# Interleaving the first two feed-forward blocks of a linear-attention and FFN kernel while its weights are converted

## The chip, the cores and the metric

One core of one Trainium2 chip. The metric is the time of one execution on the device in microseconds (us), as the median of several runs. Some executions of a kernel can be slower, at a lower clock. Each experiment ran on one chip with runs of the kernel before; not all used the same chip. The *granted clock* is the share of TensorE's full clock that the profile shows as granted to it. A ratio is the mean time of one kernel's fast runs over that of the other's of the same rounds, so it is not quite the ratio of the medians quoted beside it; the interval is 95%.

## The reference

```python
# attention: batch 4, heads 8, seq 768, head_dim 48
f = 1.0 / (1.0 + np.exp(-f_logit))
for t in range(S):
    state = f[:, :, t, :, None] * state + np.einsum('bhd,bhe->bhde', k[:, :, t], v[:, :, t])
    y[:, :, t] = np.einsum('bhd,bhde->bhe', q[:, :, t], state)
# feed-forward: 3072 tokens, d_model 384, d_ff 1536
a = x @ w_a
b = x @ w_b
return (a * b @ w_out).astype(np.float32)      # x is y, heads side by side
```

The three weights arrive in double precision and are brought to single precision on the chip.

## The kernel before

The names that matter. A *block* is 384 tokens; there are eight. A *unit* is four heads of a block; units 0 and 1 make block 0, and so on up to unit 15. The weights come in 36 *pieces* of 128 x 384: twelve of w_b and twelve of w_a in turn, then twelve of w_out. A piece passes ScalarE and GpSimd, then four instructions on VectorE. An *input set* holds the input tiles of one unit. A feed-forward block has twelve *up steps* (b-half, a-half, product `ab` on VectorE), each of which needs one piece of w_b and one of w_a, and then three *down groups* of twelve matmuls, which need w_out. (Each matmul makes two records in a profile. In the kernel before, block 0 takes the 36 down matmuls as twelve groups of three instead.) In the code NFT is 12 and NTG is 3, so a block has 15 steps.

A unit passes through `front` (three parts, split by `yield`: ScalarE and GpSimd; long scans on VectorE; short scans and the products of q and k on VectorE), `scores` (48 small matmuls that need the scaled k, then a mask on VectorE), `turn`, `gains`, `within` and `across`. Instructions stand on each engine in program order, so the text below is the schedule. From unit 2 on a `slot` spreads these parts between the up steps and down groups:

```python
def slot(u):
    nxt = front(u + 1) if u + 1 < NU else iter(())
    if u > NQ:                   # NQ = 2
        within(u - 1)
    if u < NU:
        scores(u)
    yield
    next(nxt, None)              # front of u + 1, first part
    yield
    if u < NU:
        turn(u)
    yield
    next(nxt, None)              # second part
    yield
    ...                          # across(u - 1), gains(u)
    yield
    next(nxt, None)              # last part: k of u + 1
    yield
```

The start and the main loop, cut:

```python
for names in ("f", "kqv"):
    for u in range(NQ):
        for n, eng, x in (("f", nc.vector, 30.0), ("k", nc.gpsimd, 0.0), ("q", nc.vector, 0.0)):
            if n in names:
                eng.memset(sets[u][n], x)
        load_unit(u, names)
for ps in (ps_x, ps_y):
    nc.vector.memset(ps, 0.0)
...                              # units 0 and 1, pieces 1 and 2, front of unit 2
convert(4)
queue = []
for s in slots:
    for d in (0, 1, 2.2, 3.4, 4.6, 5.8)[1 if s == NQ else 0:]:
        queue.append(((s - NQ) * (NFT + NTG) / 2 - 6 + d, s))      # one slot in 7.5 steps
queue.sort(reverse=True)
for blk in range(NBLK):
    for i in range(10**6):
        step = blk * (NFT + NTG) + (min(i, NFT) + max(i - NFT, 0) / 4 if blk == 0 else i)
        while queue and queue[-1][0] <= step:
            next(slots[queue.pop()[1]], None)
        if i == 0:
            part = ffn(blk)      # one up step or down group at each next(part)
        if blk == 0:
            convert(min(2 * i + 4, 2 * NFT) if i < NFT - 1 else NFT + i + 3)
        if next(part, "end") == "end":
            break
```

So block 0 alone runs during the conversion; its down groups follow the pieces of w_out one by one.

## Time and profile before

| | before |
|---|---|
| time, median of 4 runs | 706.44 us (706.01 to 706.95) |
| span of the profiled run, granted TensorE clock | 703.4 us, 0.968 |
| last piece of w_out converted | 159.5 us |
| TensorE gapless from | 163.06 us |

The page's slices, the busy time by stretch and the end of the first stage are shown in the prediction. The timeline of TensorE in the kernel before, scores alone (start, length, engine, line, operation, tiles, shapes, count; in brackets the idle time before it and what ended it):

```profile
42.85 1.66 PE L277 MATMUL ps_x<-q_in,k_in 48*64 48x64 f32 x48 [8.48 <-DVE k_in L249]
60.14 0.88 PE L277 MATMUL ps_x<-q_in,k_in 48*64 48x64 f32 x48
108.04 1.56 PE L277 MATMUL ps_x<-q_in,k_in 48*64 48x64 f32 x48 [7.12 <-DVE k_in L249]
167.73 0.88 PE L277 MATMUL ps_x<-q_in,k_in 48*64 48x64 f32 x48
198.88 0.93 PE L277 MATMUL ps_x<-q_in,k_in 48*64 48x64 f32 x48
```

Units 2 and 4 find TensorE waiting; unit 3 and those from 5 on do not. Where it waited, the 48 matmuls take 1.6 us instead of 0.9: they run at half the clock (from 108.04 to 109.53 us the granted clock is 0.50).

### The profile page before, as it was taken

How to read it: one execution, taken by the hardware profiler on the slowest of the kernel's cores; microseconds unless marked ns; L12 is line 12 of the kernel's file. 1: busy time of each engine (PE TensorE's matmuls, PEld its weight loads, DVE VectorE, ACT ScalarE, POOL GpSimd, SP SyncE). 2: the span in 40 equal slices, each digit the busy share in tenths (PEclk: the TensorE clock that was granted, in tenths of full speed). 3: DMA queues.
4: the chain of work that ended last, by engine and by line, in shares of the span. 5: the costliest groups of instructions: out<-in, count | busy, mean ns of one | idle time of the engine just before them, and what ended most of it. 6: DMA issues, size and time to landing. Idle time of an engine off the chain costs nothing.

```text
span 703.4 us, 11473 instructions
## 1 busy us (share of the span) xinstructions
PE 640.7 (91%) x4770; PEld 389.9 (55%) x4770; DVE 278.9 (40%) x566; ACT 177.9 (25%) x343; POOL 76.2 (11%) x110
## 2 busy tenths in 40 slices
PE   1519868789999999999999999999999999999996
PEld 1415435346666666666666656566666665555553
DVE  8679999994343124231434024231514111001100
ACT  2543665652221022112121122112121021101100
POOL 6333443530000000000000000000000000000000
PEclk9858988999999999999999999999999999999999
DMA  9972365451030403040121203040000000000000
GB/s 205 234 202 69 112 171 143 131 132 55 10 77 18 101 1 86 1 107 12 32 55 48 71 1 86 0 107 12 18 2 29 23 1 18 20 33 0 1 12 26
DMA packets 34301, 43.30 MB, mean 62 GB/s; under 512 B 4032, under 2 KB 32704, under 8 KB 34240
## 3 DMA queue, kind: packets, MB, share of 16 engines
q1 hardware_dynamic: 24224, 29.60, 16.9%
q10 hardware_dynamic: 10016, 12.88, 6.2%
q8 instruction: 39, 0.64, 0.4%
q14 instruction: 22, 0.18, 0.1%
HBM read 33.03 MB, written 4.72 MB: 54 GB/s over the span
## 4 chain that ended last, share of the span: by engine, by line
PE 78%; DVE 13%; DMA 4%; ACT 2%; issue 1%; ACTq 1%; POOL 0%; SPq 0%; DVEq 0%; POOLq 0%
PE f L418 48%; PE f L438 24%; DVE r L193 3%; DVE h L189 2%; DVE r L192 2%; DVE f_in L237 1%; PE ps_y L356 1%; PE ps_y L376 1%; PE ps_x L277 1%; PE ps_x L304 1%; DMA raw<-in_moe_w_b_dram 1%; PE ps_x L323 1%; DVE w_b L195 1%; DVE inv L247 1%; DMA v_in<-in_v_dram 1%
## 5 line engine op out<-in xcount | busy, mean ns | idle before, releaser
L418 PE MATMUL f<-xT,w_b 128*128 128x384 f32 x576 | 209.7, 501 | 6.9 <-ACT b_sb L426 6.9
L418 PE MATMUL f<-xT,w_a 128*128 128x384 f32 x576 | 202.6, 488 | 0.0
L438 PE MATMUL f<-w_out,ab 128*128 128x384 f32 x576 | 192.1, 492 | 5.9 <-ACT b_sb L426 3.0
L428 DVE TENSOR_TENSOR ab<-f,b_sb 128x384 f32<-128x384 f32 x96 | 53.5, 557 | 308.8 <-PE f L418 307.6
L438 PEld LDWEIGHTS f<-w_out,ab 128*128 128x128 f32 x576 | 109.2, 191 | 83.7 <-DVE w_out L195 5.4
L418 PEld LDWEIGHTS f<-xT,w_a 128*128 128x128 f32 x576 | 110.5, 192 | 77.7 <-issue 2.4
L418 PEld LDWEIGHTS f<-xT,w_b 128*128 128x128 f32 x576 | 108.3, 194 | 78.7 <-ACT b_sb L426 9.8
L426 ACT COPY b_sb<-f 128x384 f32<-128x384 f32 x96 | 46.0, 479 | 243.3 <-PE f L418 236.3
L448 ACT COPY o_sb<-f 128x384 f32<-128x384 f32 x24 | 11.5, 479 | 175.3 <-PE f L438 173.9
L232 POOL TENSOR_SCALAR inv<-inv 128x768 f32<-128x768 f32 x16 | 15.0, 937 | 369.2 <-ACT inv L230 369.2
L277 PE MATMUL ps_x<-q_in,k_in 48*64 48x64 f32 x720 | 15.7, 239 | 30.0 <-DVE k_in L249 15.6
L183 POOL TENSOR_SCALAR h<-h 128x384 f32<-128x384 f32 x36 | 25.9, 720 | 66.5 <-ACT h L177 66.0
L277 PEld LDWEIGHTS ps_x<-q_in,k_in 48*64 48x64 f32 x720 | 13.9, 151 | 30.8 <-DVE k_in L249 15.9
L237 DVE TENSOR_TENSOR_SCAN f_in<-f,zero 128x384 f32<-128x384 f32 x32 | 29.9, 974 | 1.7 <-ACT inv L230 1.7
L339 DVE TENSOR_TENSOR st<-st,ps_x 128x96 f32<-128x96 f32 x80 | 20.3, 253 | 24.3 <-PE ps_x L323 21.8
L177 ACT ACTIVATE h<-raw 128x384 f32<-128x384 f32 x36 | 20.0, 557 | 38.5 <-DVE r L193 24.8
L387 ACT COPY y<-ps_y 64x384 f32<-64x384 f32 (+1 forms) x48 | 22.8, 475 | 18.5 <-PE ps_y L376 16.0
L184 POOL TENSOR_SCALAR h<-h 128x384 uint16<-128x384 uint16 x36 | 27.0, 751 | 3.0
L247 DVE TENSOR_TENSOR_SCAN inv<-inv,start,zero 128x128 f32<-128x128 f32 x64 | 26.9, 461 | 0.0
L193 DVE SCALAR_TENSOR_TENSOR r<-raw,r 128x384 f32<-128x384 uint32 x36 | 24.8, 690 | 1.2
L180 ACT ACTIVATE bit<-sign 128x384 uint16<-128x384 f32 x36 | 22.9, 636 | 1.3
L189 DVE SCALAR_TENSOR_TENSOR h<-h,bit 128x384 uint32<-128x384 uint32 x36 | 21.0, 584 | 1.3 <-POOL h L184 1.3
(60 smaller groups left out, 303.0 us busy)
## 6 DMA issues: line engine op xcount, KB each, us to landing
f_in<-in_f_logit_dram SPq DMA_DIRECT2D x32, 144.0 KB, 3.0
k_in<-in_k_dram SPq DMA_DIRECT2D x32, 144.0 KB, 3.5
q_in<-in_q_dram SPq DMA_DIRECT2D x32, 144.0 KB, 3.9
v_in<-in_v_dram SPq DMA_DIRECT2D x16, 288.0 KB, 4.3
raw<-in_moe_w_out_dram ACTq DMA_DIRECT2D x12, 384.0 KB, 3.1
out_dram<-o_sb SPq DMA_DIRECT2D x24, 192.0 KB, 1.9
raw<-in_moe_w_b_dram ACTq DMA_DIRECT2D x10, 384.0 KB, 3.5
raw<-in_moe_w_a_dram ACTq DMA_DIRECT2D x10, 384.0 KB, 3.3
```

What stands on the lines that cost most here:

```text
L180: nc.scalar.activation(bit.bitcast(U16).rearrange("p (n two) -> p n two", two=2)[:, :, 1], sign, AF.Relu, scale=-32768.0)
L183: nc.gpsimd.tensor_scalar(h, h, HI_MAX, HI_MIN, ALU.min, ALU.max)
L184: nc.gpsimd.tensor_scalar(upper, upper, 1.0, -float(HI_BIAS), ALU.mult, ALU.add)
L189: nc.vector.scalar_tensor_tensor(out=hu, in0=hu, scalar=3, in1=bit, op0=ALU.logical_shift_left, op1=ALU.bitwise_or)
L193: nc.vector.scalar_tensor_tensor(out=r, in0=lo, scalar=2.0**-52, in1=r, op0=ALU.mult, op1=ALU.mult)
L237: nc.vector.tensor_tensor_scan(x[:, c], f[:, c], none, math.exp(MIDDLE), ALU.mult, ALU.add)
L247: nc.vector.tensor_tensor_scan(inv[:, w], inv[:, w], none[:, 0:C], first, ALU.mult, ALU.add)
L277: nc.tensor.matmul(ps[h][SUB * p:SUB * p + SUB, o:o + SUB], lhsT=kf[r, tokens(n, c, p)], rhs=qf[r, tokens(n, c, p)], start=True, stop=True,)
L418: nc.tensor.matmul(ps[nm], lhsT=w[:, kt, ft * 128:ft * 128 + 128], rhs=x[:, kt], start=kt == 0, stop=kt == NKT - 1,)
L426: nc.scalar.copy(b_sb, ps["b"])
L428: nc.vector.tensor_tensor(ab[ft], ps["a"], b_sb, ALU.mult)
L438: nc.tensor.matmul(o[tg], lhsT=ab[ft][:, tg * 128:tg * 128 + 128], rhs=w_out[:, ft], start=ft == 0, stop=ft == NFT - 1,)
```

## The change

Its intent is to run up steps of blocks 0 and 1 in turn while pieces are converted, so that two converted columns of w_a and w_b serve two up steps instead of one and TensorE has work during the conversion of w_out. For it, units 2 and 3 (block 1) move ahead, units 4 to 6 get slots at steps 12, 18 and 24, three input sets take the place of four (with single buffers for `at`, `kT`, `y`, to make room for more `ab`), and the start gives VectorE's clearing to GpSimd and ScalarE. Cut to its core:

```diff
-    NSET = 4
+    NSET = 3
...
-        for ps in (ps_x, ps_y):
-            nc.vector.memset(ps, 0.0)
+        for n, x in (("f", 30.0), ("k", 0.0), ("q", 0.0)):
+            for u in range(NSET):
+                eng = nc.vector if n == "f" or n == "q" and u == 0 else nc.gpsimd
+                eng.memset(sets[u][n], x)
+        for ps in (ps_x, ps_y):
+            nc.scalar.copy(ps[:, :, 0:BLK], zero.unsqueeze(1).broadcast_to((128, 2, BLK)))
...
         across(1)
+        convert(4)
+        up(0, 0)
         next(fronts[2])
         next(fronts[2])
-        slots = {s: slot(s) for s in range(NQ, NU + 1)}
-        next(slots[NQ])
-        convert(4)
+        next(fronts[3])
+        next(fronts[3])
+        scores(2)
+        turn(2, True)
+        within(2)
+        next(fronts[3])
+        gains(2)
+        up(0, 1)
+        scores(3)
+        across(2)
+        turn(3, True)
+        convert(6)
+        up(0, 2)
+        within(3)
+        gains(3)
+        convert(8)
+        up(0, 3)
+        across(3)
+        convert(10)
+        up(0, 4)
+        rest = [(up, blk, i + 5 * (1 - blk)) for i in range(7) for blk in (1, 0)]
+        rest += [(up, 1, i) for i in range(7, NFT)]
+        rest += [(down, blk, tg) for blk in range(2) for tg in range(NTG)]
...                                  # then blocks 2 to 7, each ups then downs
+        first = {2 * NQ: 12, 2 * NQ + 1: 18}
+        queue = [(2 * NQ + 5, fronts[2 * NQ]), (2 * NQ + 6.5, fronts[2 * NQ]), (2 * NQ + 7.5, fronts[2 * NQ])]
         for s in slots:
-            for d in (0, 1, 2.2, 3.4, 4.6, 5.8)[1 if s == NQ else 0:]:
-                queue.append(((s - NQ) * (NFT + NTG) / 2 - 6 + d, s))
+            for d in (0, 1, 2.2, 3.4, 4.6, 5.8):
+                queue.append((first.get(s, (s - NQ) * (NFT + NTG) / 2 - 6) + d, slots[s]))
...
+        for step, (what, blk, i) in enumerate(rest, 5):
+            while queue and queue[-1][0] <= step:
+                next(queue.pop()[1], None)
+            convert(10 + (step - 4) * 3 // 2)
+            what(blk, i)
```

More of the change, by code (lines that the diff above doesn't have):

```diff
@@ L89, in by_quotients @@
     NBLK = B * NH
-    NSET = 4
+    NSET = 3
     fixedp = ctx.enter_context(tc.tile_pool(name="fixed", bufs=1))
+    sb1 = ctx.enter_context(tc.tile_pool(name="sb1", bufs=1))
     sb2 = ctx.enter_context(tc.tile_pool(name="sb2", bufs=2))
-    sb4 = ctx.enter_context(tc.tile_pool(name="sb4", bufs=4))
-    ab_pool = ctx.enter_context(tc.tile_pool(name="ab", bufs=NFT + 1))
+    sb3 = ctx.enter_context(tc.tile_pool(name="sb3", bufs=3))
+    ab_pool = ctx.enter_context(tc.tile_pool(name="ab", bufs=2 * NFT + 1))
     raw_pool = ctx.enter_context(tc.tile_pool(name="raw", bufs=5))
@@ L114, in by_quotients @@
     less = fixed([128, 1], "less")
-    signs = [
-        (fixed([128, PIECE], f"sign{i}"), fixedp.tile([128, PIECE], U32, tag=f"bit{i}", name=f"bit{i}"))
-        for i in range(3)
-    ]
+    sign = fixed([128, PIECE], "sign")
+    bits = [fixedp.tile([128, PIECE], U32, tag=f"bit{i}", name=f"bit{i}") for i in range(3)]
     tails = fixed([128, NU], "tails")
@@ L171, in from_double @@
         lo, hi = words[:, :, 0], words[:, :, 1]
-        i = nth[0] % len(signs)
+        bit = bits[nth[0] % len(bits)]
         nth[0] += 1
-        sign, bit = signs[i]
-        h = sb4.tile([128, PIECE], FP32, tag="h", name="h")
+        h = sb3.tile([128, PIECE], FP32, tag="h", name="h")
         upper = h.bitcast(U16).rearrange("p (n two) -> p n two", two=2)[:, :, 1]
@@ L206, in conversion, with rounds @@
                     going.remove(g)
-            if n:
+            if n > 1:
                 load_weights()
-            yield n - 1
+            yield
     ready = conversion()
     def convert(n):
-        while done[0] < min(n, len(todo)):
-            done[0] = next(ready)
+        rounds(min(n, len(todo)) + 2)
+    def rounds(n):
+        while done[0] < n:
+            next(ready)
+            done[0] += 1
     live = {}
@@ L283, in scores @@
                     )
-        at = sb2.tile([128, 2, BLK], FP32, tag="at", name="at")
+        at = sb1.tile([128, 2, BLK], FP32, tag="at", name="at")
         both = [(at[:, h], ps[h][:, 0:BLK]) for h in range(2)] if spare else [(at, ps_x[:, :, 0:BLK])]
@@ L298, in turn @@
         kf = halves(sets[u % NSET]["k"])
-        kT = sb2.tile([128, 2, NC, 128], FP32, tag="kT", name="kT")
+        kT = sb1.tile([128, 2, NC, 128], FP32, tag="kT", name="kT")
         ps = pair(spare)
@@ L329, in gains @@
                         )
-        st = sb4.tile([128, NJ, 2, D], FP32, tag="st", name="st")
+        st = sb3.tile([128, NJ, 2, D], FP32, tag="st", name="st")
         before = live[u - NQ]["st"][NJ] if half else None
@@ L383, in across @@
                     )
-        y = sb2.tile([128, 2 * NC, 2, SUB], FP32, tag="y", name="y")
+        y = sb1.tile([128, 2 * NC, 2, SUB], FP32, tag="y", name="y")
         for p, e, r, rows in ((0, 0, 0, 128), (1, R, 0, R), (1, 0, R, R)):
@@ L406, in across @@
         load_unit(u + NSET)
-    def ffn(blk):
-        x = xT.pop(blk)
-        ab = []
-        for ft in range(NFT):
-            yield
-            ps = {}
-            for nm, w in (("b", w_b), ("a", w_a)):
-                ps[nm] = ps_f.tile([128, 512], FP32, tag="f", name="f")[:, 0:BLK]
-                for kt in range(NKT):
-                    nc.tensor.matmul(
-                        ps[nm],
-                        lhsT=w[:, kt, ft * 128:ft * 128 + 128],
-                        rhs=x[:, kt],
-                        start=kt == 0,
-                        stop=kt == NKT - 1,
-                    )
-            b_sb = sb2.tile([128, BLK], FP32, tag="b_sb", name="b_sb")
-            nc.scalar.copy(b_sb, ps["b"])
-            ab.append(ab_pool.tile([128, BLK], FP32, tag="ab", name="ab"))
-            nc.vector.tensor_tensor(ab[ft], ps["a"], b_sb, ALU.mult)
-        o = [ps_f.tile([128, 512], FP32, tag="f", name="f")[:, 0:DM] for _ in range(NTG)] if blk == 0 else []
-        order = [[(tg, ft) for tg in range(NTG)] for ft in range(NFT)] if blk == 0 else []
-        order = order or [[(tg, ft) for ft in range(NFT)] for tg in range(NTG)]
-        for group in order:
-            yield
-            for tg, ft in group:
-                if tg == len(o):
-                    o.append(ps_f.tile([128, 512], FP32, tag="f", name="f")[:, 0:DM])
-                nc.tensor.matmul(
-                    o[tg],
-                    lhsT=ab[ft][:, tg * 128:tg * 128 + 128],
-                    rhs=w_out[:, ft],
-                    start=ft == 0,
-                    stop=ft == NFT - 1,
-                )
-                if ft < NFT - 1:
-                    continue
-                o_sb = sb2.tile([128, DM], FP32, tag="o_sb", name="o_sb")
-                nc.scalar.copy(o_sb, o[tg])
-                r0 = blk * BLK + tg * 128
-                nc.sync.dma_start(out=out[r0:r0 + 128], in_=o_sb)
@@ new lines, in by_quotients, with up @@
+    abs_ = {blk: [] for blk in range(NBLK)}
+    def up(blk, ft):
+        x, ab, ps = xT[blk], abs_[blk], {}
+        for nm, w in (("b", w_b), ("a", w_a)):
+            ps[nm] = ps_f.tile([128, 512], FP32, tag="f", name="f")[:, 0:BLK]
+            for kt in range(NKT):
+                nc.tensor.matmul(
+                    ps[nm],
+                    lhsT=w[:, kt, ft * 128:ft * 128 + 128],
+                    rhs=x[:, kt],
+                    start=kt == 0,
+                    stop=kt == NKT - 1,
+                )
+        b_sb = sb2.tile([128, BLK], FP32, tag="b_sb", name="b_sb")
+        nc.scalar.copy(b_sb, ps["b"])
+        ab.append(ab_pool.tile([128, BLK], FP32, tag="ab", name="ab"))
+        nc.vector.tensor_tensor(ab[ft], ps["a"], b_sb, ALU.mult)
@@ new lines, in down @@
+    def down(blk, tg):
+        o = ps_f.tile([128, 512], FP32, tag="f", name="f")[:, 0:DM]
+        for ft in range(NFT):
+            nc.tensor.matmul(
+                o,
+                lhsT=abs_[blk][ft][:, tg * 128:tg * 128 + 128],
+                rhs=w_out[:, ft],
+                start=ft == 0,
+                stop=ft == NFT - 1,
+            )
+        o_sb = sb2.tile([128, DM], FP32, tag="o_sb", name="o_sb")
+        nc.scalar.copy(o_sb, o)
+        r0 = blk * BLK + tg * 128
+        nc.sync.dma_start(out=out[r0:r0 + 128], in_=o_sb)
@@ L452, in slot @@
     def slot(u):
         nxt = front(u + 1) if u + 1 < NU else iter(())
-        if u > NQ:
+        if u > 2 * NQ:
             within(u - 1)
@@ L466, in slot @@
         yield
-        if u > NQ:
+        if u > 2 * NQ:
             across(u - 1)
@@ L491, in by_quotients @@
             nc.gpsimd.memset(x, value)
-        for names in ("f", "kqv"):
-            for u in range(NQ):
-                for n, eng, x in (("f", nc.vector, 30.0), ("k", nc.gpsimd, 0.0), ("q", nc.vector, 0.0)):
-                    if n in names:
-                        eng.memset(sets[u][n], x)
-                load_unit(u, names)
-        for ps in (ps_x, ps_y):
-            nc.vector.memset(ps, 0.0)
+        for n, x in (("f", 30.0), ("k", 0.0), ("q", 0.0)):
+            for u in range(NSET):
+                eng = nc.vector if n == "f" or n == "q" and u == 0 else nc.gpsimd
+                eng.memset(sets[u][n], x)
+        for ps in (ps_x, ps_y):
+            nc.scalar.copy(ps[:, :, 0:BLK], zero.unsqueeze(1).broadcast_to((128, 2, BLK)))
+        load_unit(0, "f")
+        load_unit(1, "f")
+        load_unit(0, "kqv")
+        load_unit(1, "kqv")
         load_weights()
         load_weights()
-        for u in range(NQ, NSET):
-            for n, eng, x in (("f", nc.gpsimd, 30.0), ("k", nc.gpsimd, 0.0), ("q", nc.vector, 0.0)):
-                eng.memset(sets[u][n], x)
-            load_unit(u)
-            load_weights()
+        load_unit(2)
+        load_weights()
+        load_weights()
         done = [0]
-        fronts = [front(u) for u in range(NQ + 1)]
+        fronts = [front(u) for u in range(2 * NQ + 1)]
         next(fronts[0])
         next(fronts[1])
-        for _, bit in signs:
+        for bit in bits:
             nc.gpsimd.memset(bit, 0)
@@ L526, in by_quotients @@
         turn(0, True)
-        convert(0)
+        rounds(1)
         next(fronts[1])
@@ L530, in by_quotients @@
         gains(0)
+        rounds(2)
         scores(1, True)
         turn(1, True)
-        convert(1)
         across(0)
         within(1)
+        rounds(3)
         gains(1)
+        rounds(4)
         next(fronts[2])
-        convert(2)
         across(1)
+        convert(4)
+        up(0, 0)
         next(fronts[2])
         next(fronts[2])
-        slots = {s: slot(s) for s in range(NQ, NU + 1)}
-        next(slots[NQ])
-        convert(4)
-        queue = []
-        for s in slots:
-            for d in (0, 1, 2.2, 3.4, 4.6, 5.8)[1 if s == NQ else 0:]:
-                queue.append(((s - NQ) * (NFT + NTG) / 2 - 6 + d, s))
@@ L551, in by_quotients @@
-        queue.sort(reverse=True)
-        for blk in range(NBLK):
-            for i in range(10**6):
-                step = blk * (NFT + NTG) + (min(i, NFT) + max(i - NFT, 0) / 4 if blk == 0 else i)
-                while queue and queue[-1][0] <= step:
-                    next(slots[queue.pop()[1]], None)
-                if i == 0:
-                    part = ffn(blk)
-                if blk == 0:
-                    convert(min(2 * i + 4, 2 * NFT) if i < NFT - 1 else NFT + i + 3)
-                if next(part, "end") == "end":
-                    break
-            if blk == NBLK - 2:
+        next(fronts[3])
@@ new lines, in by_quotients @@
+        rest += [(down, blk, tg) for blk in range(2) for tg in range(NTG)]
+        for blk in range(2, NBLK):
+            rest += [(up, blk, ft) for ft in range(NFT)] + [(down, blk, tg) for tg in range(NTG)]
+        slots = {s: slot(s) for s in range(2 * NQ, NU + 1)}
+        first = {2 * NQ: 12, 2 * NQ + 1: 18}
+        queue = [(2 * NQ + 5, fronts[2 * NQ]), (2 * NQ + 6.5, fronts[2 * NQ]), (2 * NQ + 7.5, fronts[2 * NQ])]
+        for s in slots:
+            for d in (0, 1, 2.2, 3.4, 4.6, 5.8):
+                queue.append((first.get(s, (s - NQ) * (NFT + NTG) / 2 - 6) + d, slots[s]))
@@ L564, in by_quotients @@
+        queue.sort(reverse=True, key=lambda x: x[0])
+        for step, (what, blk, i) in enumerate(rest, 5):
[3 more added lines that the diff above has]
+            what(blk, i)
+            if (what, blk, i) == (down, NBLK - 2, NTG - 1):
                 check_held()
+        for _, s in reversed(queue):
+            next(s, None)
 def by_levels(ctx, tc, q, k, f_logit, v, masks, out, ident, weights):
```

## The prediction

> **What bounds the kernel now.** I read the page's 40 slices first, to see where the limits change; then the busy time by stretch, cut at the places where they change; then the waits of the first 170 us and the timeline there. The slices (17.6 us each):
>
> ```profile
> PE   1519868789999999999999999999999999999996
> DVE  8679999994343124231434024231514111001100
> ```
>
> VectorE is full from slice 2 to slice 9 (some 35 to 160 us), TensorE from slice 9 on. By stretch (columns: stretch, length, busy us of PE, PEld, DVE, ACT, POOL, then granted clock, DMA share, GB/s):
>
> ```profile
> 61.00:152.00 91.00, 72.92 (x478) 41.84 (x475) 86.19 (x151) 59.09 (x113) 43.14 (x60) 0.92 0.46 135
> ...
> 170.00:690.00 520.00, 520.00 (x3560) 315.41 (x3559) 131.40 (x288) 91.81 (x180) 8.34 (x10) 1.00 0.13 33
> ```
>
> In the first stretch VectorE works 86 of 91 us and TensorE 73; in the second TensorE works 520.00 of 520: no gap. So the time is the moment at which VectorE ends the conversion of the 36 weight pieces, plus the TensorE work still left then, plus a tail of 6 us (last PE end 697.24, span 703.4). A change gains only if, when the conversion ends, less TensorE work is left per microsecond of delay. Where the first stage ends:
>
> ```profile
> 158.95 0.56 DVE L195 TENSOR_TENSOR w_out<-h,r 128x384 f32<-128x384 f32 x1
> ...
> 163.06 2.10 PE L418 MATMUL f<-xT,w_b 128*128 128x384 f32 x6
> ...
> 165.00 2.10 PE L418 MATMUL f<-xT,w_a 128*128 128x384 f32 x6
> ...
> 167.20 0.56 DVE L428 TENSOR_TENSOR ab<-f,b_sb 128x384 f32<-128x384 f32 x1 [3.76 <-PE f L418]
> ```
>
> Conversion ends at 159.5, block 0 at 163.06, and from there TensorE runs gapless to 697.24. The lines also give the units: half an up step (one weight, three k tiles) is 165.00 - 163.06 = 1.94, an up step 3.88, a down group of 12 matmuls 7.76 (same matmul), a block 12 x 3.88 + 3 x 7.76 = 69.8 us. From the start of an a-half to its product on VectorE are 167.20 - 165.00 = 2.2 us. The costs on VectorE, from the groups (mean ns before the bar):
>
> ```profile
> L428 DVE TENSOR_TENSOR ab<-f,b_sb 128x384 f32<-128x384 f32 x96 | 53.5, 557 | 308.8 <-PE f L418 307.6
> L193 DVE SCALAR_TENSOR_TENSOR r<-raw,r 128x384 f32<-128x384 uint32 x36 | 24.8, 690 | 1.2
> L189 DVE SCALAR_TENSOR_TENSOR h<-h,bit 128x384 uint32<-128x384 uint32 x36 | 21.0, 584 | 1.3 <-POOL h L184 1.3
> ```
>
> With L192 (426) and L195 (690 over its three outputs) a piece is 0.584 + 0.426 + 0.690 + 0.690 = 2.39 us. A unit's front (two long scans 1.95, held and reciprocal 0.38, six short scans 2.66, two products 1.88) is 6.87, a mask 0.96, states 1.3 to 2.0, a product ab 0.557. Check: between the fifth piece (59.6) and the last (159.5) VectorE did 32 pieces 76.5, 12 ab 6.7, two masks 1.9, states 3.3, a front and the scans of another 9.0, in all 97.4 in 99.9 us: factor 1.026, so it waited for next to nothing. TensorE's waits in this stretch are for VectorE, directly or through ScalarE:
>
> ```profile
> PE ps_x L277 <- DVE k_in L249: 7.1, 1, 7.1
> PE f L418 <- ACT b_sb L426: 6.9, 5, 2.2
> ```
>
> **What the Trainium skill says.** "Perfetto Trace Analysis", Optimization Strategy: where the most contended engine changes over time, interleaving the regimes may help. This is the change's idea, and the two regimes are in the slices above. "TensorE: Matmul & The Clock Gate", What's actually happening: after an idle window of about 3.4 us TensorE runs at half clock until a busy one. The trace agrees: the first b-half, at 53.59 after idling, took 3.8 us instead of 1.94. "SBUF — State Buffer", Who interferes with whom: VectorE instructions with two SBUF inputs contend with GpSimd's reads. It agrees in kind: L193 took 0.56 in some pieces and 0.81 in others. "DMA: Bandwidth & Descriptors", Issuing engines are not separate DMA queues: transfers of both queues interleave on the same engines. The xT transfers landed after 5.1 us (median) in the first 60 us, 2.1 later.
>
> **Part by part**, from the orders of instructions of the two kernels.
>
> 1. Start. VectorE loses four memsets of 0.7 and two PSUM clears of 0.91 (to GpSimd and ScalarE, idle there). The first scan starts when ScalarE is done, 6.3 instead of 7.93; I get the second k product at 19.4 instead of 21.1, and y of unit 0 near 23.5 instead of 28.2, as it is no longer behind a piece on ScalarE. Gain 2 to 4 us at this point.
>
> 2. The order of the first four units. Up step (0,0) now stands before unit 2 on TensorE, and its ab before unit 2's front on VectorE. Its xT needs y of unit 1: ScalarE y ends near 34, three DMA issues 2, landing 2 to 5: 38 to 41. Then 5.9 us at low clock (53.59 to 59.44 before): ab near 45. VectorE has finished pieces 1 to 4 near 37.5, so it idles some 7 us. After it: ab 0.6, front 5.9, scans of the next 2, mask 1, rest of the front 3.9, state 1.4, wait for up step (0,1) 1.8, its ab and a mask 1.5: the fifth piece starts near 63.5 instead of 59.6. For that VectorE has two ab and a mask more behind it (2.1).
>
> 3. Up steps (0,2), (0,3), (0,4) directly follow their own two pieces, where before the conversion was two to four pieces ahead. VectorE's next instruction is ab, which needs the a-half, which needs the piece just made: 3 x 2.2 = 6.7 us idle, plus 0.9 for unit 3's state and 1.6 for steps (1,0) and (1,1). Two masks that now directly follow their k product: 2 x 1.1.
>
> 4. Interleaving. Before the last piece there are now 22 ab instead of 12, a second whole front, its mask and the scans of a third. From the fifth piece on: 32 pieces 76.5, 20 ab 11.1, fronts 13.7 + 2.2, masks 1.9, states 3.3 = 108.7, x 1.026 = 111.5, plus the idle time of part 3 (11.4): 63.5 + 122.9 = 186 us; walking it instruction by instruction I get 185. In exchange TensorE has then begun the 24th up step. Two weight columns now serve 7.76 us of TensorE work against 2 pieces and 2 ab = 5.9 us.
>
> 5. What is left. At 184.4 TensorE starts the last up step: 188.3; unit 5's attention 0.9; then the scores of unit 6 wait for the front that VectorE gets to after ab: until 193.8, 4.6 us idle; scores 0.9: 194.7. Left: 6 down groups 46.6, six blocks 418.8, attention of ten units 42 (4.2 each by the groups' busy times; checked on 163.06 to 697.24 this way of adding is 0.45% high). (46.6 + 418.8 + 42) x 0.9955 = 505.1, so TensorE ends at 699.8 against 697.24: 2.6 us later.
>
> 6. Three sets, one buffer for at, kT, y, one sign tile. A unit's load starts after across of three units before, 3.9 steps ahead of its sigmoid: 15 us at 3.88 a step, and y copies, five issues and landing take some 10. No cost in the full stretch. Sign is written and read by ScalarE alone. Three h buffers hold ScalarE back by one L195, but raw transfers are asked for one piece later, which lets b_sb go earlier; I take both as zero.
>
> **The rivals.** (a) The interleaving works as meant: the stalls of part 3 vanish, for instance because the b_sb copies come earlier and TensorE is ahead. Then conversion ends 11 us earlier: 698. For it: TensorE has slack in the stage (73 of 91 us before). Against: the order on VectorE is fixed, and an ab cannot be passed. (b) Low clock makes the stalls double: a-halves after gaps take 3.8 instead of 1.94, the first xT lands late: 6 to 8 us more, 716. For it: the granted clock was 0.92 in the stage and 0.67 from 50 to 61. (c) The later start of loads stalls TensorE in the full stretch: 14 units x 1 us, 720. Against: the slack of 5 us in part 6.
>
> **Range and chances.** Working: 706.6 + 2.6 = 709; low clock adds a little; the case that it is a kept step of tuning, so that some stall is smaller than I think, takes off a little more. I say 708. The idle times I worked out for VectorE total some 34 us against 17 before; an error of a third of that is 10 us either way: 698 to 717. Faster by over 2% (below 692.5) would need VectorE idle less than before: 0.07. Slower by over 2% (above 720.8) needs (b) and (c): 0.06.
>
> **What would show it.** Right: VectorE idles 5 to 9 us before the first ab; gaps of some 2 us before the next ab; fifth piece near 63.5; last piece at 180 to 190; 4 to 5 us on the scores of unit 6; no gap after 200. Wrong: VectorE without those gaps (then faster), or TensorE gaps after 200 on loads (then slower).

## The result and the profile after

| | before | after | predicted for after |
|---|---|---|---|
| time, median of 4 runs | 706.44 | 716.90 (715.63 to 717.40) | 708 (698 to 717) |
| ratio to before | | 1.0145 (1.0127 to 1.0163) | |
| span of the profiled run, clock | 703.4, 0.968 | 713.9, 0.956 | |
| fifth piece begun | 59.6 | 63.97 | 63.5 |
| last piece converted | 159.5 | 189.26 | 185 to 186 |
| TensorE gapless from | 163.06 | 198.57 | 193.8 |
| end of TensorE | 697.24 | 707.9 | 699.8 |

The change is 1.5% slower: within the 2% that counts as the same, but outside the noise. The slices of the page after (TensorE, VectorE, and the granted clock in tenths):

```profile
PE   1638697887989999999999999999999999999996
DVE  7867579898820213314251215221331311001100
...
PEclk9668899797989999999999999999999999999999
```

VectorE now has a hollow in slices 2 to 5 and stays busy (7 to 9 tenths) until slice 10. TensorE, which before had nines from slice 9 on, has only 8, 8 and 7 in slices 7 to 9 and an 8 in slice 11, and in 7, 9 and 11 the clock falls too (slices counted from 0). The stretches that the prediction showed of before, now of after:

```profile
61.00:152.00 91.00, 72.56 (x520) 42.64 (x522) 71.74 (x128) 49.69 (x98) 33.34 (x48) 0.91 0.49 133
170.00:690.00 520.00, 516.17 (x3536) 313.26 (x3535) 142.68 (x306) 95.33 (x188) 14.48 (x18) 0.99 0.15 38
```

In the same 91 us VectorE did 71.7 us of work, not 86.2, and TensorE no more than before. The interleaving was to give TensorE more to do here; what it did instead was to wait. The scores in TensorE's timeline after:

```profile
52.91 1.56 PE L279 MATMUL ps_x<-q_in,k_in 48*64 48x64 f32 x48 [6.92 <-DVE k_in L251]
62.10 0.93 PE L279 MATMUL ps_x<-q_in,k_in 48*64 48x64 f32 x48
128.39 1.56 PE L279 MATMUL ps_x<-q_in,k_in 48*64 48x64 f32 x48 [8.72 <-DVE k_in L251]
164.75 1.56 PE L279 MATMUL ps_x<-q_in,k_in 48*64 48x64 f32 x48 [7.62 <-DVE k_in L251]
198.57 1.66 PE L279 MATMUL ps_x<-q_in,k_in 48*64 48x64 f32 x48 [3.83 <-DVE k_in L251]
```

Now units 4, 5 and 6 all wait, for 20.2 us in all after 100 us, where before there was one wait of 7.1. The reason is in the order. The last part of a front is at offset 5.8 of the slot before, and slots 4, 5 and 6 are 6 steps apart instead of 7.5; unit 4's front is queued by itself, with its last part at 11.5 and its scores at 12. So there is no up step left between a unit's k on VectorE and its scores on TensorE, and TensorE has nothing else to go on with. (In the kernel before, one up step stood between for unit 4, and it waited 7.1 us all the same: VectorE was that far behind.) What follows on TensorE shows the second cost:

```profile
128.39 1.56 PE L279 MATMUL ps_x<-q_in,k_in 48*64 48x64 f32 x48 [8.72 <-DVE k_in L251]
129.88 3.61 PE L418 MATMUL f<-xT,w_b 128*128 128x384 f32 x6
133.32 2.10 PE L418 MATMUL f<-xT,w_a 128*128 128x384 f32 x6
...
166.24 4.20 PE L418 MATMUL f<-xT,w_b 128*128 128x384 f32 x6
...
200.16 5.27 PE L434 MATMUL f<-w_out,ab 128*128 128x384 f32 x9
```

A half (the matmuls of an up step for one weight) that takes 2.10 us takes 3.6 to 4.2 directly after such a wait, and the first nine records of the down groups after the last wait take 5.27 us; at full clock nine take 2.9 (72 take 23.38 at the end of the kernel). On VectorE, the waits for a product or for the scores are (timeline of VectorE after, those with idle time before them):

```profile
46.10 0.56 DVE L428 TENSOR_TENSOR ab<-f,b_sb 128x384 f32<-128x384 f32 x1 [6.51 <-PE f L418]
...
70.94 0.56 DVE L428 TENSOR_TENSOR ab<-f,b_sb 128x384 f32<-128x384 f32 x1 [2.36 <-PE f L418]
...
82.88 0.56 DVE L428 TENSOR_TENSOR ab<-f,b_sb 128x384 f32<-128x384 f32 x1 [5.15 <-PE f L418]
90.65 0.56 DVE L428 TENSOR_TENSOR ab<-f,b_sb 128x384 f32<-128x384 f32 x1 [2.37 <-PE f L418]
94.97 0.56 DVE L428 TENSOR_TENSOR ab<-f,b_sb 128x384 f32<-128x384 f32 x1 [1.43 <-PE f L418]
...
166.38 0.96 DVE L295 TENSOR_TENSOR at<-ps_x,causal 128x768 f32<-128x768 f32 x1 [1.68 <-PE ps_x L279]
```

The costs of the single VectorE instructions changed little: `ab` has a mean of 557 ns in both kernels, a long scan 974 before and 1007 after. Nor does anything come after the first stage: from 201 to 690 us TensorE works 489.00 of 489 us in both.

### The profile page after: what moved, and what is told of

It is laid out like the page before. It is cut to its first block, busy times and chain, and to the rows that moved or that the text cites. A ratio compares the mean times of both kernels' runs of the same rounds, so it can differ in the third digit from the quotient of the medians.

```text
span 713.9 us, 11434 instructions
## 1 busy us (share of the span) xinstructions
PE 645.6 (90%) x4770; PEld 394.6 (55%) x4770; DVE 275.8 (39%) x562; ACT 178.0 (25%) x347; POOL 71.5 (10%) x109
## 4 chain that ended last, share of the span: by engine, by line
PE 83%; DVE 12%; DMA 2%; issue 1%; ACT 1%; SPq 0%; ACTq 0%; DVEq 0%
PE f L418 49%; PE f L434 27%; PE ps_x L279 2%; DVE inv L249 2%; DVE r L191 2%; PE ps_y L378 2%; PE ps_y L358 1%; DVE f_in L239 1%; DMA xT<-y 1%; DVE h L187 1%; PE ps_x L325 1%; DVE r L190 1%; PE ps_x L306 1%; DVE ab L428 1%; DVE k_in L251 1%
## 5 line engine op out<-in xcount | busy, mean ns | idle before, releaser
L418 PE MATMUL f<-xT,w_b 128*128 128x384 f32 x576 | 212.0, 505 | 14.4 <-DMA xT<-y 6.8
L442 ACT COPY o_sb<-f 128x384 f32<-128x384 f32 x24 | 11.5, 479 | 183.6 <-PE f L434 142.0
L279 PE MATMUL ps_x<-q_in,k_in 48*64 48x64 f32 x720 | 17.5, 252 | 41.8 <-DVE k_in L251 27.1
L279 PEld LDWEIGHTS ps_x<-q_in,k_in 48*64 48x64 f32 x720 | 15.4, 163 | 44.3 <-DVE k_in L251 28.6
L239 DVE TENSOR_TENSOR_SCAN f_in<-f,zero 128x384 f32<-128x384 f32 x32 | 30.9, 1007 | 14.5 <-ACT inv L232 14.5
L181 POOL TENSOR_SCALAR h<-h 128x384 f32<-128x384 f32 x36 | 20.8, 578 | 101.3 <-ACT h L175 101.0
```

Of the source, the lines that this page charges most:

```text
L239: nc.vector.tensor_tensor_scan(x[:, c], f[:, c], none, math.exp(MIDDLE), ALU.mult, ALU.add)
L279: nc.tensor.matmul(ps[h][SUB * p:SUB * p + SUB, o:o + SUB], lhsT=kf[r, tokens(n, c, p)], rhs=qf[r, tokens(n, c, p)], start=True, stop=True,)
L418: nc.tensor.matmul(ps[nm], lhsT=w[:, kt, ft * 128:ft * 128 + 128], rhs=x[:, kt], start=kt == 0, stop=kt == NKT - 1,)
```

## The experiments

All edits are to the changed kernel unless another is named. Twelve kernels ran, all correct. The landmarks are from the profiled runs. Kernels of different calls are compared below by their medians; by their ratios to the kernel before, such differences come out up to 1.8 us larger or smaller.

| kernel | median | before | ratio (95%) | last piece done | first down group |
|---|---|---|---|---|---|
| after | 716.90 | 706.44 | 1.0145 | 189.3 | 200.2 |
| e1_ahead | 714.74 | 705.63 | 1.013 (1.0106 to 1.0154) | 182.7 | 198.8 |
| e2_up00_later | 714.07 | 705.63 | 1.0116 (1.0091 to 1.0142) | 187.9 | 198.8 |
| e3_units_later | 692.04 | 705.63 | 0.9805 (0.9778 to 0.9831) | 172.2 | 170.6 |
| e4_in_turn | 724.34 | 706.73 | 1.0247 (1.0224 to 1.0269) | 192.3 | 208.3 |
| e5_three_sets | 704.68 | 705.63 | 0.9984 (0.9961 to 1.0007) | | |
| e6_all | 688.05 | 706.73 | 0.9741 (0.9725 to 0.9757) | 161.0 | 166.3 |
| e7_fronts_sooner | 701.84 | 706.73 | 0.9934 (0.9917 to 0.995) | 190.1 | 188.2 |
| e8_later_in_turn | 702.65 | 706.73 | 0.9948 (0.9932 to 0.9965) | 182.2 | 180.5 |
| e9_warm | 710.55 | 706.41 | 1.0061 (1.0044 to 1.0078) | 185.5 | 195.5 |
| e10_fill | 681.83 | 706.41 | 0.9652 (0.9623 to 0.9681) | 154.7 | 160.0 |
| e11_start | 705.12 | 706.41 | 0.9976 (0.996 to 0.9993) | | |
| e12_in_stage | 691.17 | 704.97 | 0.9806 (0.9786 to 0.9826) | 176.8 | 177.3 |

### e1_ahead: pieces one step earlier

My first theory was the prediction's own: VectorE sets the end of the stage, and the direct dependence of an up step on its own two pieces costs it idle time. So each step's pieces are converted one piece sooner.

```diff
-        convert(6)
+        convert(7)
         up(0, 2)
...                          # likewise 8 to 9 and 10 to 11
-            convert(10 + (step - 4) * 3 // 2)
+            convert(11 + (step - 4) * 3 // 2)
```

> The changed kernel with the conversion one piece further ahead of the up steps. Theory (VectorE idles because ab directly follows the pieces it depends on): the gaps of 2.36, 5.15, 2.37 and 1.43 us before the four ab between 64 and 98 us shrink to under 0.5 each, with the half-clock matmuls that they cause; the last piece ends some 8 to 11 us earlier than 189, time 706 to 709. Rival (the low clock of TensorE itself is the cause, whatever the order): the gaps stay at about half or more, time 713 or above.

Measured: 714.74. VectorE's four gaps went from 11.3 to 5.4 us in all, not to under 0.5 each (1.88, 1.56, 0.23 and 1.77 in the trace), while TensorE's wait for unit 4's k grew from 8.72 to 10.40. The last piece came 6.6 us sooner, the time only 2.2. So the last piece isn't what ends the stage: the first down group began at 198.8 instead of 200.2, since scores of unit 6 stand before it and wait for their k as before. The theory that the conversion alone sets the end fell here.

### e2_up00_later: the first up step after unit 2's scores

```diff
         convert(4)
-        up(0, 0)
...
         next(fronts[3])
+        up(0, 0)
         gains(2)
```

> The changed kernel with up step (0,0) moved behind unit 2's scores, turn and within, its ab behind both fronts. Theory (the 6.5 us of VectorE before the first ab are only a matter of order): the gap disappears, the fifth piece starts at 57 to 59 instead of 64, time 710 to 712. Rival (unit 3's data or ScalarE isn't ready any earlier, so the wait only moves): the fifth piece starts at 62 or later, time 715 to 717.

Measured: 714.07. The idle time of 6.51 us ahead of the first `ab` became 2.40 there and 2.72 at the next: it mostly moved. The fifth piece began 0.6 us sooner; what more was gained by the first down group (1.4 us in all) came at up steps (0,3) and (1,0), whose waits were 4.43 and 0.96 us instead of 5.15 and 1.43. The rival was right for the most part.

### e3_units_later: units 4 to 6 out of the stage

The slots of units 4, 5 and 6 move behind the up steps, between half down groups, where VectorE is nearly free (unit 4's front stands among the last up steps).

```diff
-        rest += [(down, blk, tg) for blk in range(2) for tg in range(NTG)]
+        rest += [(down, blk, tg, part) for blk in range(2) for tg in range(NTG) for part in range(2)]
...
-        first = {2 * NQ: 12, 2 * NQ + 1: 18}
-        queue = [(2 * NQ + 5, fronts[2 * NQ]), (2 * NQ + 6.5, fronts[2 * NQ]), (2 * NQ + 7.5, fronts[2 * NQ])]
+        first = {2 * NQ: 24, 2 * NQ + 1: 26, 2 * NQ + 2: 28}
+        queue = [(x, fronts[2 * NQ]) for x in (20, 21, 22)]
...
-            for d in (0, 1, 2.2, 3.4, 4.6, 5.8):
+            for d in (0, 0, 0.5, 0.5, 1, 1) if s in first else (0, 1, 2.2, 3.4, 4.6, 5.8):
```

> The changed kernel with units 4, 5 and 6 moved out of the conversion to the down groups of blocks 0 and 1. Theory (VectorE's extra attention work, 14 us, and TensorE's waits of 8.7, 7.6 and 3.8 us for k products are what the interleaving costs): last piece ends at 172 to 176 instead of 189, no wait for k products above 2 us after 100, and as some 8 us of attention on TensorE come later, time 702 to 707. Rival (TensorE lacks that work in the conversion and block 2 waits for its xT): no gain, 714 or more, with a gap of several us before block 2.

Measured: 692.04, 24.9 us under the changed kernel and better than my expectation. Busy time in the stretch in which the waits were, after and then with this edit:

```profile
98.00:201.00 103.00, 82.71 (x600) 50.55 (x601) 90.10 (x170) 49.84 (x98) 32.58 (x47) 0.88 0.34 96
```

```profile
98.00:201.00 103.00, 100.09 (x580) 59.52 (x581) 84.78 (x158) 51.61 (x101) 31.81 (x47) 1.00 0.29 89
```

TensorE works 100 of 103 us instead of 83, at full instead of 0.88 clock. The edit does two things: it takes VectorE work from the stage, and it takes away the waits. e7_fronts_sooner, e10_fill and e12_in_stage tell them apart.

### e7_fronts_sooner: the same units in the same stage, fronts ahead of their scores

Only the order within the slots of units 4 to 6 changes: each front ends three up steps ahead of its scores. No work moves out of the stage.

```diff
-        queue = [(2 * NQ + 5, fronts[2 * NQ]), (2 * NQ + 6.5, fronts[2 * NQ]), (2 * NQ + 7.5, fronts[2 * NQ])]
+        queue = [(x, fronts[2 * NQ]) for x in (7, 8, 9)]
         for s in slots:
-            for d in (0, 1, 2.2, 3.4, 4.6, 5.8):
+            for d in (0, 1, 1, 2, 3, 3) if s in first else (0, 1, 2.2, 3.4, 4.6, 5.8):
```

> The changed kernel with the same units in the conversion, but each front finished two or three steps before its scores. Theory A (order: TensorE waits because scores directly follow the front): the waits of 8.7, 7.6 and 3.8 us mostly vanish, 700 to 706. Theory B (work: VectorE has 14 us more to do in the stage, whatever its place, and idles only some 8 us of the last 100): the waits move to weight pieces, 711 to 716.

Measured: 701.84, 15.1 us under the changed kernel and 0.7% under the kernel before. VectorE ends the pieces at 190.1, no sooner than in the changed kernel, and yet the down groups begin at 188.2 instead of 200.2. The scores of units 4 to 6 in TensorE's timeline:

```profile
121.58 0.93 PE L279 MATMUL ps_x<-q_in,k_in 48*64 48x64 f32 x48
156.61 0.88 PE L279 MATMUL ps_x<-q_in,k_in 48*64 48x64 f32 x48
187.38 0.92 PE L279 MATMUL ps_x<-q_in,k_in 48*64 48x64 f32 x48
188.22 22.20 PE L434 MATMUL f<-w_out,ab 128*128 128x384 f32 x68
```

None of these scores waits, and none is slow. TensorE isn't without waits: its others after 100 us sum to 10.7 us (the longest 2.35, followed by one half of 3.68), against 20.2 for k alone in the changed kernel. This shows the main cause of the change's loss: the order of fronts and scores in its stage.

### e9_warm: TensorE kept at work during the waits

How much of the loss is the waiting, and how much the half clock after it? Here the waits stay, but TensorE passes them with matmuls of no use.

```diff
         if u > 2 * NQ:
             within(u - 1)
+        for _ in range({4: 30, 5: 26, 6: 12}.get(u, 0)):
+            nc.tensor.matmul(ps_x[:, 0, 384:512], lhsT=ident, rhs=xT[1][:, 0, 0:128], start=True, stop=True)
         if u < NU:
             scores(u)
```

> The changed kernel with small matmuls of no use (identity by a slice of the second input tile, into an unused part of the score tile's bank) before the scores of units 4, 5 and 6, so that TensorE works while it waits for the scaled k. Theory: the half-speed time after those waits is a by-cost: the mask waits of 1.7 us go to 1.1 and the down-slot's next up halves from 3.4 to 4.2 us to 1.94, but VectorE and the order still set when the stage ends: 712 to 715. Rival (the clock is the bulk of the miss): 710 or less. If the added matmuls delay the scores: 717 or more.

Measured: 710.55, 6.4 us under the changed kernel. I had expected 712 to 715; the rival's line was 710 or less, and the result is nearer to it. TensorE's timeline around the scores of unit 4:

```profile
128.19 0.93 PE L279 MATMUL ps_x<-q_in,k_in 48*64 48x64 f32 x48 [1.95 <-DVE k_in L251]
129.05 2.20 PE L418 MATMUL f<-xT,w_b 128*128 128x384 f32 x6
```

At this point the two traces differ by 0.2 us (128.19 and 128.39). The scores of unit 5 then begin 1.4 us sooner, those of unit 6 4.0, the down groups 4.7, and TensorE ends at 701.1 instead of 707.9. So the half clock after three waits cost 6.8 us in the traces. (By difference, an estimate: of the 15.1 us that e7_fronts_sooner gains, some 6 are clock and the rest the waiting itself.) That is most of what the prediction was too low by: it had put the down groups at 194.7 and TensorE's end at 699.8, and this kernel has 195.5 and 701.1.

### e4_in_turn and e8_later_in_turn: is the interleaving itself worth anything?

e4 is e1_ahead, and e8 is e3_units_later, each with the up steps of the two blocks one block after the other.

```diff
-        rest = [(up, blk, i + 5 * (1 - blk)) for i in range(7) for blk in (1, 0)]
-        rest += [(up, 1, i) for i in range(7, NFT)]
+        rest = [(up, 0, i) for i in range(5, NFT)] + [(up, 1, i) for i in range(NFT)]
...                          # pieces 2 i + 3 before up(0, i) at the latest
```

> The kernel of e1_ahead with the two blocks' up steps one block after the other instead of interleaved. Theory (in the changed kernel the interleaving gains nothing, as the stage is set by the units' fronts on VectorE and by TensorE waiting for them): within 4 us of e1_ahead, 711 to 718. Rival (the interleaving carries the stage): 722 or more.

> The kernel of e3_units_later, up steps one block after the other. Theory (with the units out of the stage the interleaving does matter: block 0 alone needs two pieces and an ab, 5.5 us of VectorE, for 3.88 us of TensorE, seven times): TensorE idle some 11 us more from 98 to 130, time 700 to 705 against 692. Rival (VectorE's sum is what counts, the order of the blocks is indifferent): 690 to 695.

Measured: 724.34 for e4, 9.6 us over e1_ahead, and 702.65 for e8, 10.6 over e3_units_later. In e4 my theory that the interleaving gains nothing fell; in e8 its value came out as expected. The timeline of TensorE in e8 shows why: with one block at a time, each half waits for its piece.

```profile
108.92 2.20 PE L418 MATMUL f<-xT,w_a 128*128 128x384 f32 x6 [0.68 <-DVE w_a L193]
111.48 2.17 PE L418 MATMUL f<-xT,w_b 128*128 128x384 f32 x6 [0.36 <-DVE w_b L193]
114.34 2.20 PE L418 MATMUL f<-xT,w_a 128*128 128x384 f32 x6 [0.68 <-DVE w_a L193]
```

An up step takes 114.34 - 108.92 = 5.42 us there, instead of 3.88. So the interleaving is worth some 10 us within the changed kernel (8 to 10 by the ratios), and the change's order spends more than that.

### e5_three_sets and e11_start: the change's side parts alone

Both are edits of the kernel before. e5 has three input sets (and one more piece loaded early); e11 has the clearing of the change's start.

```diff
-    NSET = 4
+    NSET = 3
...                          # e5; and one more load_weights() at the start
```

```diff
-        for ps in (ps_x, ps_y):
-            nc.vector.memset(ps, 0.0)
+        for n, x in (("f", 30.0), ("k", 0.0), ("q", 0.0)):
+            for u in range(NSET):
+                eng = nc.vector if n == "f" or n == "q" and u == 0 else nc.gpsimd
+                eng.memset(sets[u][n], x)
+        for ps in (ps_x, ps_y):
+            nc.scalar.copy(ps[:, :, 0:BLK], zero.unsqueeze(1).broadcast_to((128, 2, BLK)))
...                          # e11; the old memsets of the sets go
```

> The kernel before with three input sets instead of four, nothing else. Theory (sets are no cost: loads have slack): 706.4 within 1.5 us, TensorE without a gap from 170 on. Rival (loads come too late): gaps on TensorE of about 1 us a unit after 170, 712 to 720.

> The kernel before with only the change's start (clearing of the SBUF tiles on GpSimd, of the PSUM banks on ScalarE). What I hold after the traces: no gain, within 1.5 us of the kernel before, as GpSimd's clearing lies beside VectorE's first passes and lengthens them. The prediction's part 1 said 2 to 4 us gained at that point: if it is right, 703 to 705.

Measured: 704.68 for e5, no difference, since 1 lies in its interval. 705.12 for e11, 0.24% under before: 1.3 us by the medians and 1.7 by the ratio, whose interval of 0.5 to 2.8 touches the prediction's 2 to 4. At the prediction's own point, though, the trace shows no gain: the second k product ends at 21.1 in both kernels. The first long scans on VectorE, before and then e11:

```profile
7.93 1.77 DVE L237 TENSOR_TENSOR_SCAN f_in<-f,zero 128x384 f32<-128x384 f32 x2
```

```profile
7.13 2.48 DVE L237 TENSOR_TENSOR_SCAN f_in<-f,zero 128x384 f32<-128x384 f32 x2 [2.18 <-ACT inv L230]
```

They begin 0.8 us sooner, but take 0.7 longer, all of it in the first scan (1.63 instead of 0.92). In e11 they begin at the same moment as GpSimd's multiply of `inv` (7.13, 0.83 us long); before, VectorE's memsets had kept them until that multiply was all but over (7.21 to 8.04). That the two engines hold each other up is inferred from this coincidence; no run moved the multiply away. GpSimd's clearing, which my expectation blamed, is over at 5.7, before the scans begin.

### e6_all, e10_fill and e12_in_stage: putting the parts together

e6_all has the edits of e1, e2 and e3. e10_fill takes e6_all and converts pieces 3 and 4 after unit 2's front and scores instead of before them, and piece 5 ahead of up step (0,1) instead of later:

```diff
-        convert(4)
         next(fronts[2])
         next(fronts[2])
         next(fronts[3])
-        next(fronts[3])
         scores(2)
         turn(2, True)
+        convert(3)
+        next(fronts[3])
         within(2)
         next(fronts[3])
+        convert(4)
         up(0, 0)
         gains(2)
+        convert(5)
         up(0, 1)
```

e12_in_stage has all of that except e3: units 4 to 6 stay in the stage, in the order of e7.

> e1, e2 and e3 together. Theory (with the units moved, VectorE's idle time between 40 and 98 us is on the path, so removing it now pays what it did not pay alone): 10 us below e3_units_later, 680 to 685. Rival (the idle only moves again): 688 to 692.

> The kernel with all three corrections (e6_all, 688.05), and pieces 3 to 5 of w_in converted after unit 2's front instead of before it, into VectorE's idle time of that stretch. Theory: VectorE's idle time is filled and the pieces still come in time: 681 to 685. Rival: the idle time moves to another place, since the pieces are what the first up steps wait for: 687 to 690.

> The change with units 4 to 6 left in the stage of conversion, as it meant them, but with the order put right: fronts ahead of their scores as in e7_fronts_sooner (701.84), pieces a step earlier (e1), first up step later (e2), pieces 3 to 5 of w_in after unit 2's front (e10). Theory: what units 4 to 6 cost in the stage beyond their bad order is their VectorE work beside the pieces, which moving them to the downs (e10_fill, 681.83) had taken away, so this stays 8 to 12 us above e10_fill: 690 to 694. Rival: the order was all of it and the place of the units does not matter: 681 to 686.

Measured: e6_all 688.05, so the two small edits are worth 4.0 us together on top of e3 (the rival was right: part of the idle time moved). e10_fill 681.83, as its theory said: VectorE's work in the first 98 us rose from 46.81 + 27.46 = 74.3 us (e6_all) to 49.74 + 30.58 = 80.3, and the time fell by 6.2. This is the fastest kernel, 3.5% under before and 4.9% under the change (681.83 / 716.90). e12_in_stage 691.17, as its theory said: with the order put right everywhere, leaving units 4 to 6 in the stage still costs 9.3 us over e10_fill (10.9 by the ratios). What lies between the changed kernel and e10_fill thus splits into some 24 to 26 us of order and 9 to 11 of place.

## Why the prediction was right or wrong

The class was right, and the time lay 8.9 us above the number named and only 0.1 us inside the range, which is luck: the range came from a third of VectorE's idle time, and what used it up was mostly TensorE's clock. By its own steps:

1. *Start, 2 to 4 us.* Failed. The second k product ended at 22.2 (predicted 19.4; before 21.1), y of unit 0 began at 26.09 (predicted 23.5; before 28.18), and in e11_start the k product ends no sooner than before. VectorE has two memsets less, not four (six before, four after). The first scan started at 7.40, when ScalarE's second pass, `inv`, was done, and not at 6.3; it then took longer beside GpSimd's multiply, as in e11; and unit 1's two products took 1.27 and 1.25 us, against 0.94 and 0.95 before, while GpSimd was at work on the first pieces.
2. *The first up step.* Right: first `ab` at 46.10 (predicted 45) after 6.51 us of idle (7), fifth piece at 63.97 (63.5).
3. *Stalls of 11.4 us.* The mechanism was right, each stall in its place, but the size was off. VectorE's idle time up to the last piece was 38.7 us (34). The waits from the fifth to the last piece sum to 18.0: that of up step (0,3) took 5.15 instead of 2.2, since its b-half ran at half clock (4.18 us), and the masks took 1.68 instead of 1.1. With TensorE kept at work in the two later waits (e9_warm), the last piece is done at 185.5, which is the prediction's 185 to 186; in the changed kernel it is 189.3. The agreement is in part chance, as e9_warm began its fifth piece at 65.2, 1.7 later than predicted.
4. *The wait at unit 6 and what is left.* The wait was there (3.83, predicted 4.6). What is left after it was 507.7 us instead of 505.1, as the first down matmuls ran at half clock; e9_warm has 505.6.
5. *Three sets.* Right: no cost, alone (e5_three_sets) or in the trace, where TensorE has no gap from 201 to 690 us. The single buffers were not run alone.

What failed in size is therefore the low clock, beside the start. The prediction named it as rival (b), "6 to 8 us more, 716", and took it into its own number with only "low clock adds a little". Of TensorE's three waits for k it gave only that of unit 6 a length; for units 4 and 5 it counted VectorE's 1.1 us at each mask, and not the 8.72 and 7.62 us that TensorE stands still before, nor the slow matmuls after. e9_warm measures the clock's part: 6.4 us in time, against a miss of 8.9. The idle window of about 3.4 us that the prediction took from the skill isn't a safe limit here either: waits of 2.18 us (before, at 76.93) and 2.35 (e7_fronts_sooner) were followed by halves of 3.48 and 3.68.

Two small readings were off: VectorE's nines stand in slices 3 to 8 (53 to 158 us), not 2 to 9, and 3 x 2.2 is 6.6. A larger point was the account of the waits. The prediction says only that TensorE's waits are for VectorE, and looks for gain and loss mainly in VectorE's idle time. e7_fronts_sooner shows what that leaves out: with the last piece no sooner, the time is 15.1 us less, because TensorE does its up steps during that time instead of after it. What counts at the end of the stage is how much TensorE has left, as the prediction itself says; a wait in program order ahead of ready work adds to that.

What stays open: whether a better place exists for the 8.67 us wait that e10_fill has ahead of unit 2's scores; and what the kernel before would gain if only its own waits for k (8.48 and 7.12 us) were put right. No run tried the second, so how much of e10_fill's 3.5% needs the interleaving of blocks is known only from the changed kernel's side (e4, e8).

## What to carry to other kernels

When work of two stages is interleaved, look first at what stands in the slower engine's way in program order: a small product placed directly behind the instruction that makes its operand stops the whole queue, and here that cost more than the interleaving gave. Put ready work between a producer and its consumer on another engine, enough for the producer's lag: one up step was too little for unit 4 in the kernel before, three were enough in e7_fronts_sooner. Move what the bound engine need not do now to a stage where it is idle. For a prediction, put the matmuls after every longer wait of TensorE at half clock (in the fourteen traces, from 35 to 220 us, waits of 3.6 us and more always did it, and those of 2 to 3 us sometimes: after the same wait of 2.04 us ahead of up step (0,4) the two halves took 2.17 and 2.20 us in the changed kernel, but 2.87 and 3.21 in e9_warm), and count the end of a stage by the work that is left, not by the last piece that is done.

## What the Trainium skill lacked or had wrong

- "TensorE: Matmul & The Clock Gate" ("HAM oscillation — how this bites in real kernels") advises to restructure the loop or pad M; neither it nor another page tells of filling a wait inside a kernel with matmuls of no use (the page warms up with matmuls for benchmarks only). Here 68 of them during three waits raised the granted clock between 98 and 201 us from 0.88 to 1.00 and took 6.4 us off. That the ramp costs under 1% of a typical kernel span ("What's actually happening") fits barely: 6.4 of 716.9 is 0.9%, for three waits alone, and that is most of this prediction's error.
- "SBUF — State Buffer", Who interferes with whom, names copies, casts, `tensor_scalar`, `tensor_tensor` and `tensor_reduce`, but not scans; whether its rule for VectorE instructions with two SBUF inputs takes them in isn't said. Two scans of which the first began together with GpSimd's multiply took 2.48 us; begun as it ended, 1.77. That the multiply is the cause is inferred.
